# Fewer, larger loads, loads moved behind a transposition, and sums one unit ahead, in a top-k attention and gated MLP kernel

## Chip, core and metric

The kernel runs on one core of a Trainium2 chip. The metric is device time in microseconds: the median of three runs for the times, and one profiled execution for the views. An engine is written as in the profile: PE is TensorE (PEld its weight loads), DVE is VectorE, ACT is ScalarE, POOL is GpSimd, SP is SyncE, which here issues nearly all DMAs (SPq is its sequencer).

## The reference

Attention over 8 batches of 8 heads, 576 positions of 64 elements. Only the 32 largest scores of each row count. The result, seen as 4608 rows of 512, goes through two matrix products with a gate between them.

```python
scores = scale * np.matmul(q, k.transpose(0, 1, 3, 2))
kth = np.partition(scores, -top_k, axis=-1)[..., -top_k:-top_k + 1]
scores = np.where(scores >= kth, scores, -1000000000.0)
attn = np.exp(scores - np.max(scores, axis=-1, keepdims=True))
attn = attn / (np.sum(attn, axis=-1, keepdims=True) + 1e-09)
attn_out = np.matmul(attn, v)
x = attn_out.transpose(0, 2, 1, 3).reshape(4608, 512)
h = x @ w_in                               # 512 -> 2048
g = h * (1.0 / (1.0 + np.exp(-1.702 * h)))
out = g @ w_out                            # 2048 -> 512
```

## The kernel before

**Slots.** The attention is cut into 144 slots, 18 for each batch. A full slot is one pair of heads (hp, 0 to 3) against 128 of the first 512 query rows; two slots of a batch hold the ends, the last 64 rows of two pairs at once. Batches of even number run their 16 full slots first and then the two slots of ends; odd ones begin with the ends. All four pairs of v are therefore read in the last two slots of an even batch and in the first two of an odd one.

**A slot's way.** PE makes the scores (L315), ACT copies them to SBUF as `sc` (copy_scores, L327). DVE halves them into pairs (pair_up, L337) and finds the 32 largest by MAX8 and MATCH_REPLACE8 (L351, L355). POOL makes bounds, ACT masks and takes exponentials into `pr` (L382, L390), DVE inverts the sums (L398, L400), POOL scales `pr` (normalize, L413). `split(n)` (L449, L451) copies `pr` on ACT into two planes of 16 bits, over the slot's own `sc`, and SP writes them to DRAM as `rows`. `turn_by_dma(n)` (L457) has SP read them back transposed as `pt`; that DMA waits until `rows` has landed and until PE has read the `pt` of two slots before, since there are two buffers. Then PE multiplies by v (`values_at`, L516), and ACT copies the result to `xT` (x_of, L530 or L533). `sc` has four buffers, so copy_scores of slot n + 4 waits until `rows` of slot n has landed.

**The MLP** runs between the slots in units of four groups of 128 hidden features: `hidden` on PE (L573), `tanh` on ACT (L589), `gate` (on POOL, or on DVE at L604 when the attention is done), `combine` (four sums for a seven-product scheme, L626 to L629) and `project` on PE (L680). The units go through lists in order of arrival: to_gate, gated, to_combine, to_project. The tiles `th`, `h` and `sums` come from one pool of eight. When a block's four units are projected, ACT takes the sums from PSUM (L698), the parts are added (L705) and SP writes four pieces to `out_dram` (L714).

**The order** is written out by hand. After an opening and the slots up to 12, `two_slots(n)` is called for n = 13, 15, ... 145; one call, a trip here, does the odd slot n and the even slot n + 1 of DVE's search, and `values_at` for slots n - 3 and n - 2. Below n = 21 (`filling`) its second loads come before the scores of n + 3; from there on they come near the end, between `split(n)` and `turn_by_dma(n)`. After the last trip, `last_units` empties the lists.

**Loads.** `at(n, fn, ...)` notes what is due at a slot; `begin(0)` in a trip runs what is due at n, between `split(n - 1)` and `turn_by_dma(n - 1)`, and `begin(1)` what is due at n + 1. All loads and the transpositions are issued by SP in that one order. A pair's q is fetched at FETCH, which from batch 2 on falls on begin(0), and its k one slot later, on begin(1): each is two transfers of 128 KB (L196), one for each head, and one of 32 KB for the ends (L199). At READY, `prepare_by_dma` has ACT copy the pair into two planes (`halves`, L264), SP write them to DRAM (`qk_rows`, L268 to L273), and SP read them back transposed as `qk_t` (L277), which the scores read. FETCH is -17, -13, -9 and -5 slots before the batch, READY -13, -9, -5 and -1, but in odd batches -3 for the last pair. v is loaded by `load_v` for one pair at a time: 256 KB into one of four buffers (L210) and two transfers of 16 KB for the ends into a tile of zeros (L218). VALUES says when: slots 0, 1, 2 and 3 of an even batch, and all four pairs at slot 2 of an odd one, which is begin(1) of the trip at its slot 1 (n = 19, 55, 91 and 127).

Of the kernel before, what the change touches and what calls it, by code (L numbers as in the profile page):

```python
# [11 lines left out]
F32 = mybir.dt.float32  # L12
# [6 lines left out]
P = 128  # L19
# [11 lines left out]
def kernel(  # L31
# [64 lines left out]
    pool = lambda name, bufs, **kw: ctx.enter_context(tc.tile_pool(name=name, bufs=bufs, **kw))  # L96
    raws = const.tile([P, RING, 2 * PIECE], U32, name="raws")
    loads = pool("loads", 1)
    vals = pool("vals", 4)
    qkt = pool("qkt", 6)  # L100
    scp = pool("scp", 4)
    prp = pool("prp", 2)
# [62 lines left out]

    qT, kT, vv = {}, {}, {}
    loaded = {}
    v_ends = [const.tile([P, 2, D], F32, name=f"v_e{i}") for i in range(NP)]
    for i, t in enumerate(v_ends):
        (nc.gpsimd if i else nc.vector).memset(t[:], 0.0)  # L170

    def stay_warm(count, of=ident[:]):

# [4 lines left out]
    def load(name, b, hp, queue=None):  # L178

        src = q if name == "q" else k  # L180
        if (b, hp) not in loaded:
            home, tag = (ptp, "pt") if b == 0 and hp % 2 else (prp, "pr") if b == 0 and hp else (loads, "qk_l")
            if b == 1 and hp % 2:
                parts = raws[:, 3, :].bitcast(F32), diagonals[:, 0, :]
                loaded[b, hp] = [x.rearrange("p (t j d) -> p t j d", j=2, d=D) for x in parts]
            else:
                t = home.tile([P, 2 * NF + 1, 2, D], F32, name="qk_l", tag=tag)
                loaded[b, hp] = [t[:, 0 : 2 * NF, :, :], t[:, 2 * NF :, :, :], t]
        t = loaded[b, hp]
        if queue is None:  # L190
            heads_of = lambda j: of_load(name, t)[:, :, j, :]
        else:
            heads_of = lambda j: heads_apart(name, t)[:, j, :, :]
        queue = queue or nc.sync
        for j in range(2):
            queue.dma_start(heads_of(j), src[b, 2 * hp + j, 0:FULL, :].rearrange("(p t) d -> p t d", t=NF))  # L196

        on = slice(0, TAIL) if name == "q" else slice(TAIL, P)
        queue.dma_start(t[1][on, 0, :, :], src[b, 2 * hp : 2 * hp + 2, FULL:S, :].rearrange("h p d -> p h d"))  # L199
# [5 lines left out]
        flat = of_load(name, t).rearrange("p t j d -> p (t j d)")  # L205
        return flat.rearrange("p (j t d) -> p j t d", j=2, t=NF)

    def load_v(b, hp):
        main = vals.tile([P, 2, NF, D], F32, name="v_l")
        nc.sync.dma_start(  # L210
            main[:].rearrange("p j t d -> p j (t d)"),
            v[b, 2 * hp : 2 * hp + 2, 0:FULL, :].rearrange("j (p t) d -> p j (t d)", t=NF),
        )


        tail = v_ends[(b * NP + hp) % len(v_ends)]
        for j in range(2):
            nc.sync.dma_start(tail[j * TAIL : (j + 1) * TAIL, j, :], v[b, 2 * hp + j, FULL:S, :])  # L218
        vv[b, hp] = main, tail

    def prepare_main(name, b, hp):
        src = loaded[b, hp]
# [522 lines left out]
    READY_1 = (-5, -5, -3, -3)  # L745
    FETCH = (-17, -13, -9, -5)
    FETCH_1 = (-11, -6, -4, -4)
    VALUES = (0, 1, 2, 3), (2, 2, 2, 2)
    by_slot = dict(enumerate([2, 2, 3, 3, 3, 3, 3, 3, 3, 3, 3, 1]))
    for n in by_slot:  # L750
        first = sum(map(len, list(by_slot.values())[:n]))
# [10 lines left out]
    for b in range(1, B):  # L762
        for hp in range(NP):
            if b > 1:
                for i, name in enumerate("qk"):
                    at(b * PER + FETCH[hp] + i, load, name, b, hp)
                at(b * PER + READY[b % 2][hp], prepare_by_dma, b, hp)
            else:
                at(b * PER + FETCH_1[hp], load_both, b, hp)
                at(b * PER + READY_1[hp], prepare_by_pe, b, hp)  # L770
            at(b * PER + VALUES[b % 2][hp], load_v, b, hp)
    unfinished = []
    early = []
    finished = []
# [36 lines left out]

    def opening():

        stay_warm(8, v_ends[0][:].rearrange("p j d -> p (j d)"))
        load("q", 0, 0, nc.sync)
        load("k", 0, 0, nc.scalar)
        for hp in range(2):
            for name in "qk":
                if hp:
                    load(name, 0, hp)  # L820
        for x in by_slot[0]:
            load_piece(x)
        prepare_first()
        scores(0)
        copy_scores(0)
        stay_warm(2)
        for name in "qk":
            prepare(name, 0, 1)
        early.extend(round_piece(x) for x in by_slot[0])
        for piece in early:  # L830
            piece["size"]()
        scores(1)
        copy_scores(1)
        prepare_rest()
        for hp in range(2, NP):
            for name in "qk":
                load(name, 0, hp)
        load_v(0, 0)
        for x in by_slot[1]:
            load_piece(x)  # L840
# [180 lines left out]
    def two_slots(n):  # L1021

        begin, prepare_some = dues(n)
        aside = n < N
        filling = n < STEADY + 8
        if live(n - 1):
            exponentials(n - 1)
        if n == STEADY:
            prepare_some()
        hidden(ps_t)  # L1030
        if n > STEADY + 2:
            hidden(ps_t)
# [12 lines left out]
        gate()  # L1045
        begin(0)
        if live(n - 1):
            turn_by_dma(n - 1)
        while turns:
            turns.pop(0)()  # L1050
        if live(n + 2):
            copy_scores(n + 2)
        if live(n):
            bounds(n)
            mask(n)
        combine()
        project_one()
        sum_weights(4)
        if live(n):
            exps(n)  # L1060
        tanh(aside)
        prepare_some()
        prepare_some()
        held = [m for m in (n - 3, n - 2) if live(m)]
        o = ps_t.tile([P, 4, P], F32, name="o", tag="tp") if held else None
        ends = [(b, hp, o[:, 2 + i, :]) for i, (b, hp) in enumerate(second_part)]
        second_part.clear()
        for what in ends:
            turn_qk_ends(*what)
        for i, m in enumerate(held):  # L1070
            values_at(m, o[:, i, :])
        if filling and held:
            x_of(held, o)
        for what in ends:
            copy_qk_ends(*what)
        if filling:
            begin(1)
        if live(n + 3):
            scores(n + 3)
        leave_all()  # L1080
        find(n + 1, 8)
        if live(n):
            normalize(n)
            split(n)
        if held and not filling:
            x_of(held, o)
        if not filling:
            begin(1)
        if live(n):
            turn_by_dma(n)  # L1090
        gate()
        if live(n + 3):
            copy_scores(n + 3)
        if live(n + 1):
            bounds(n + 1)
        sum_weights(4)
# [11 lines left out]
    with tc.manual_schedule():  # L1108
# [3 lines left out]
        first_pair(PAIRED)  # L1112
        for n in range(STEADY, N + 2, 2):
            two_slots(n)
        while ready or to_gate or gated or to_combine or to_project:
            last_units()
        merge_all(nc.vector)
# [30 lines left out]
```

## Time and profile before

| | us |
|---|---|
| median of three runs | 1448.03 (1445.33 to 1450.77) |
| profiled execution, its own time | 1444.36 |
| its span, first to last instruction | 1442.4 |
| PE busy in the span | 1380.9 |
| DVE busy | 1343.8 |
| ACT busy | 1163.7 |
| POOL busy | 959.3 |

The page's 40 slices show PE and DVE at nine tenths or more from about 250 us on, and the last two slices with PE alone. A row of waits names the engine that stood, the line that it stood before, what ended the wait, the total in us, the number of times and the longest. In a timeline a row has start, length, engine, line and what is written and read; for SP the length is the time to issue, and the landing is told apart. The page's part on DMAs gives the median from issue to landing: 3.6 us for `rows`, 4.9 for `pt`, 5.4 for `qk_t`, 3.8 for 256 KB of v, 3.4 to 3.5 for 128 KB of q or k.

### The profile page before, as it was taken

What the parts mean: (1) busy time and instruction counts of PE and PEld (TensorE: products, weight loads), DVE (VectorE), ACT (ScalarE), POOL (GpSimd) and SP (SyncE); (2) the same over time, 40 slices, a digit from 0 to 9 for tenths busy, and PEclk for the clock granted to TensorE, in tenths of its full rate; (3) what the DMA queues carried; (4) which work ended last, traced back from release to release, by engine and by line L of the source; (5) the groups of instructions that cost most, each with busy time, mean ns of one, the idle gap of its engine ahead of it and who ended that gap; (6) DMA issues with size and microseconds to landing.
All of it is one profiled execution on the core that took longest, in us unless ns stands there. A gap on an engine that the chain in (4) does not pass through costs nothing. (4 is left out here: it accounts for less than half of the span.)

```text
span 1442.4 us, 45910 instructions
## 1 busy us (share of the span) xinstructions
PE 1380.9 (96%) x18164; PEld 1234.5 (86%) x18164; DVE 1343.8 (93%) x3521; ACT 1163.7 (81%) x1896; POOL 959.3 (67%) x1608
## 2 busy tenths in 40 slices
PE   6889799999999999999999999999999999999996
PEld 5667478899999899899899999889999998899986
DVE  7999998999999999999999999999999999999812
ACT  6998777888888888888888898888888888888811
POOL 4787676677777667666677767667777767777710
PEclk8899899999999999999999999999999999999999
DMA  7452456777787786777787786787798877655520
GB/s 225 137 156 67 132 146 149 193 191 192 181 203 193 176 217 168 175 190 188 186 212 190 189 197 169 190 196 191 183 203 195 191 184 182 173 141 141 140 58 16
DMA packets 535991, 245.47 MB, mean 170 GB/s; under 512 B 458976, under 2 KB 514272, under 8 KB 535776
## 3 DMA queue, kind: packets, MB, share of 16 engines
q1 hardware_dynamic: 535344, 242.25, 67.1%
q8 instruction: 142, 2.33, 0.7%
q14 instruction: 73, 0.60, 0.1%
q10 hardware_dynamic: 432, 0.30, 0.1%
HBM read 45.09 MB, written 103.42 MB: 103 GB/s over the span
## 5 line engine op out<-in xcount | busy, mean ns | idle before, releaser
L351 DVE MAX8 top<-ranked 128x8 f32<-128x288 f32 (+1 forms) x1080 | 598.8, 596 | 0.0
L573 PEld LDWEIGHTS ph<-xT,win 128*128 128x128 f32 x4384 | 496.0, 193 | 30.6 <-issue 17.4
L573 PE MATMUL ph<-xT,win 128*128 128x128 f32 x4384 | 509.7, 278 | 0.0
L355 DVE MATCH_REPLACE8 ranked<-top,ranked 128x288 f32<-128x288 f32 (+1 forms) x810 | 433.5, 543 | 0.0
L413 POOL TENSOR_SCALAR pr<-pr,rden 128x576 f32<-128x576 f32 x268 | 197.0, 745 | 337.7 <-DVE rden L400 156.3
L449 ACT COPY sc<-pr 128x2304 uint16<-128x2304 uint16 x134 | 283.4, 2115 | 140.5 <-POOL pr L413 140.2
L337 DVE TENSOR_TENSOR ranked<-sc 128x576 f32<-128x576 f32 x270 | 219.6, 854 | 11.4 <-ACT sc L327 11.4
L390 ACT ACTIVATE pr<-sc,low 128x576 f32<-128x576 f32 x288 | 220.3, 773 | 0.0
L382 ACT ACTIVATE sc<-sc,cut 128x576 f32<-128x576 f32 x288 | 207.9, 779 | 4.5 <-POOL cut L369 4.5
L680 PE MATMUL po<-wout,h 128*64 128x128 f32 x2064 | 200.7, 273 | 0.2
L680 PE MATMUL po<-raws,h 128*64 128x128 f32 x2064 | 200.6, 273 | 0.2 <-POOL h L627 0.2
L327 ACT ACTIVATE sc<-s_ps 128x576 f32<-128x576 f32 x288 | 171.5, 650 | 26.2 <-DMA rows<-sc 19.1
L315 PE MATMUL s_ps<-qk_t 64*64 64x288 f32 x2304 | 181.3, 429 | 1.1 <-DMA qk_t<-qk_rows 0.8
L602 POOL TENSOR_TENSOR th<-th,h 128x512 f32<-128x512 f32 x131 | 167.7, 1280 | 10.9
L680 PE MATMUL po<-wout,th 128*64 128x128 f32 x2176 | 168.6, 276 | 0.0
L516 PE MATMUL o<-pt,v_l 128*64 128x128 f32 (+1 forms) x2400 | 146.0, 266 | 12.2 <-DMA pt<-rows 12.2
L680 PEld LDWEIGHTS po<-wout,th 128*64 128x64 f32 x2176 | 124.3, 137 | 28.4 <-issue 15.3
L516 PEld LDWEIGHTS o<-pt,v_l 128*64 128x64 f32 x2400 | 127.8, 140 | 14.2 <-issue 8.6
L680 PEld LDWEIGHTS po<-wout,h 128*64 128x64 f32 x2064 | 130.3, 137 | 0.9 <-POOL h L628 0.9
L680 PEld LDWEIGHTS po<-raws,h 128*64 128x64 f32 x2064 | 130.4, 137 | 0.6 <-POOL h L627 0.4
L315 PEld LDWEIGHTS s_ps<-qk_t 64*64 64x64 f32 x2304 | 77.1, 136 | 50.4 <-issue 14.8
L705 POOL TENSOR_TENSOR raws<-raws 128x128 f32<-128x128 f32 (+1 forms) x165 | 92.0, 566 | 37.1 <-ACT raws L698 29.3
(106 smaller groups left out, 1720.4 us busy)
## 6 DMA issues: line engine op xcount, KB each, us to landing
rows<-sc SPq DMA_DIRECT2D x134, 576.0 KB, 3.6
qk_rows<-halves SPq DMA_DIRECT2D x48, 256.0 KB, 2.9
out_dram<-raws SPq DMA_DIRECT2D x136, 64.0 KB, 2.3
raws<-in_moe_w_in_dram SPq DMA_DIRECT2D x16, 512.0 KB, 4.5
v_l<-in_v_dram SPq DMA_DIRECT2D x32, 256.0 KB, 3.8
raws<-in_moe_w_out_dram SPq DMA_DIRECT2D x16, 512.0 KB, 3.5
qk_l<-in_q_dram SPq DMA_DIRECT2D x60, 128.0 KB, 3.4
qk_l<-in_k_dram SPq DMA_DIRECT2D x58, 128.0 KB, 3.5
```

The lines of the kernel that those rows point to most:

```text
L315: nc.tensor.matmul(ps[i][rows, c, 0:HALF], lhsT=qT[b, hps[p]][on, cols], rhs=kT[b, hps[p]][on, FIRST[i] + c * HALF : FIRST[i] + (c + 1) * ...
L327: nc.scalar.mul(out=to, in_=ps[i][:, :, 0:HALF], mul=SCALE)
L337: nc.vector.tensor_tensor(out=ranked[n][:, :, c, :], in0=a, in1=b, op=op)
L351: nc.vector.max(top[:, i, 8 * r : 8 * r + 8], of(r, i))
L355: nc.vector.match_replace(to, top[:, i, 8 * r : 8 * r + 8], of(r, i), LOWEST)
L382: nc.scalar.activation(sc[:, i, :], sc[:, i, :], AF.Prelu, bias=cut[:, i : i + 1], alpha=HUGE)
L390: nc.scalar.activation(pr[:, i * S : (i + 1) * S], sc[:, i, :], AF.Exp, bias=low[:, i : i + 1], accum_out=den[:, i : i + 1],)
L413: nc.gpsimd.tensor_scalar(pr[:, i, :], pr[:, i, :], st[n]["rden"][:, i : i + 1], 1.0, op0=ALU.mult, op1=ALU.mult)
L449: nc.scalar.copy(out=halves, in_=pr[:].bitcast(U16).rearrange("p (k h) -> p h k", h=2))
L516: nc.tensor.matmul(o[j * D : (j + 1) * D, cols], lhsT=main[:, j, c, :] if c < NF else tail[:, j, :], rhs=pt[:, MAIN[j] + c if c < NF else ...
L573: nc.tensor.matmul(ph[:, i * P : (i + 1) * P], lhsT=win[:, c, f * P : (f + 1) * P], rhs=xs[:, x.place, c, :], start=(c == 0), stop=(c == C ...
L680: nc.tensor.matmul(both_banks[y * TAIL : (y + 1) * TAIL, bank, r * P : (r + 1) * P], lhsT=a[:, i, :], rhs=weight(w, fs[i])[:, y * P : (y + ...
```

## The change

- `load_v` takes several pairs. v lies in one constant tile, `v_main`, for all four pairs, the ends in one tile `v_tail`. One main transfer and two for the ends serve all pairs named. VALUES loads pairs 0 and 1 at slot 0 and 2 and 3 at slot 2 of an even batch, and all four at slot 2 of an odd one. In batch 0 the pairs are still loaded one by one.
- `load` for batches 2 and later moves q or k of both heads by one transfer of 256 KB in place of two of 128 KB. The transfer for the ends stays.
- In `two_slots`, from n = 21 on, `turn_by_dma(n)` comes before `begin(1)` and no longer after it.
- One `combine()` stands before the loop over `last_units`.

In all SP issues 102 transfers fewer. The instructions of the other engines are the same; in the tail the added `combine` moves DVE's sums one unit ahead of its gates.

```diff
-    vals = pool("vals", 4)
+    v_main = const.tile([P, NP, 2, NF, D], F32, name="v_l")
...
-    v_ends = [const.tile([P, 2, D], F32, name=f"v_e{i}") for i in range(NP)]
-    for i, t in enumerate(v_ends):
-        (nc.gpsimd if i else nc.vector).memset(t[:], 0.0)
+    v_tail = const.tile([P, NP, 2, D], F32, name="v_e")
+    for i in range(NP):
+        (nc.gpsimd if i else nc.vector).memset(v_tail[:, i, :, :], 0.0)
...
-        for j in range(2):
-            queue.dma_start(heads_of(j), src[b, 2 * hp + j, 0:FULL, :].rearrange("(p t) d -> p t d", t=NF))
+        if b > 1:
+            both = src[b, 2 * hp : 2 * hp + 2, 0:FULL, :].rearrange("j (p t) d -> p t j d", t=NF)
+            queue.dma_start(of_load(name, t), both)
+        else:
+            for j in range(2):
+                queue.dma_start(heads_of(j), src[b, 2 * hp + j, 0:FULL, :].rearrange("(p t) d -> p t d", t=NF))
...
-    def load_v(b, hp):
-        main = vals.tile([P, 2, NF, D], F32, name="v_l")
+    def load_v(b, *hps):
+        pairs, heads = slice(hps[0], hps[-1] + 1), slice(2 * hps[0], 2 * hps[-1] + 2)
         nc.sync.dma_start(
-            main[:].rearrange("p j t d -> p j (t d)"),
-            v[b, 2 * hp : 2 * hp + 2, 0:FULL, :].rearrange("j (p t) d -> p j (t d)", t=NF),
+            v_main[:, pairs, :, :, :].rearrange("p h j t d -> p (h j) (t d)"),
+            v[b, heads, 0:FULL, :].rearrange("j (p t) d -> p j (t d)", t=NF),
         )
-        tail = v_ends[(b * NP + hp) % len(v_ends)]
         for j in range(2):
-            nc.sync.dma_start(tail[j * TAIL : (j + 1) * TAIL, j, :], v[b, 2 * hp + j, FULL:S, :])
-        vv[b, hp] = main, tail
+            nc.sync.dma_start(
+                v_tail[j * TAIL : (j + 1) * TAIL, pairs, j, :],
+                v[b, heads.start + j : heads.stop : 2, FULL:S, :].rearrange("h p d -> p h d"),
+            )
+        for hp in hps:
+            vv[b, hp] = v_main[:, hp, :, :, :], v_tail[:, hp, :, :]
...
-    VALUES = (0, 1, 2, 3), (2, 2, 2, 2)
+    VALUES = {(0, 1): 0, (2, 3): 2}, {(0, 1, 2, 3): 2}
...
-            at(b * PER + VALUES[b % 2][hp], load_v, b, hp)
+        for hps, n in VALUES[b % 2].items():
+            at(b * PER + n, load_v, b, *hps)
...
         if held and not filling:
             x_of(held, o)
+        if live(n):
+            turn_by_dma(n)
         if not filling:
             begin(1)
-        if live(n):
-            turn_by_dma(n)
...
         for n in range(STEADY, N + 2, 2):
             two_slots(n)
+        combine()
         while ready or to_gate or gated or to_combine or to_project:
             last_units()
```

More of the change, by code (lines that the diff above doesn't have):

```diff
@@ L812, in opening @@
     def opening():
-        stay_warm(8, v_ends[0][:].rearrange("p j d -> p (j d)"))
+        stay_warm(8, v_tail[:, 0, :, :].rearrange("p j d -> p (j d)"))
         load("q", 0, 0, nc.sync)
```

## The prediction

> **What bounds the kernel now.** I read the page's busy shares first, then its chain of waits, the busy time by stage, the waits by engine, and last the timeline of SP's queue around them. In the fence are the page's first part, the chain's shares and one stage of 100 us (length, then PE, weight loads, DVE, ACT, POOL, granted clock, DMA share, GB/s):
>
> ```profile
> PE 1380.9 (96%) x18164; PEld 1234.5 (86%) x18164; DVE 1343.8 (93%) x3521; ACT 1163.7 (81%) x1896; POOL 959.3 (67%) x1608
> PE ph L573 6%; PE po L680 5%; PE o L516 2%; PE s_ps L315 1%; DMA pt<-rows 0%; DVE top L351 0%; DVE ranked L355 0%; ACT th L589 0%; DVE th L604 0%; DMA qk_l<-in_k_dram 0%; ACT pr L390 0%; POOL raws L705 0%; ACT sc L449 0%; ACT sc L382 0%; DVE ranked L337 0%
> 300.00:400.00 100.00, 100.00 (x1377) 91.65 (x1376) 99.62 (x266) 87.80 (x138) 70.58 (x125) 1.00 0.77 189
> ```
>
> The chain reaches back to 1176 us, and 14 of its 18 per cent are PE. In the steady part PE and DVE are both full at a granted clock of 1.00. A trip of two_slots takes PE 7.34 (ph) + 6.26 (po) + 2.18 (o) + 2 x 1.13 (s_ps) = 18.04 us by the chain of waits, and DVE has 0.4 us free in 100. So neither makes good a stall, and the end is PE's own work plus PE's waits, each of which the next view shows (engine, waited for: us, times, longest):
>
> ```profile
> PE o L516 <- DMA pt<-rows: 12.2, 7, 4.2
> PE po L680 <- DVE sums L627: 6.8, 5, 1.4
> PE s_ps L315 <- DMA qk_t<-qk_rows: 0.8, 1, 0.8
> ACT sc L327 <- DMA rows<-sc: 19.1, 13, 5.1
> ACT halves L264 <- DMA qk_l<-in_k_dram: 5.8, 3, 3.6
> ```
>
> The seven waits for pt stand at 255.90 (4.16), 494.03 (0.88), 587.17 (2.45), 698.22 (0.76), 916.30 (1.03), 955.14 (2.20) and 1247.47 (0.76). Each is for the odd slot of a trip in which loads stood in SP's queue between rows<-sc and the transposition. At 587 the queue shows it:
>
> ```profile
> 569.37 0.58 SPq L451 DMA_DIRECT2D rows<-sc  x1
> 570.00 0.43 SPq L210 DMA_DIRECT2D v_l<-in_v_dram  x1
> ...
> 578.81 1.26 SPq L196 DMA_DIRECT2D qk_l<-in_k_dram  x2
> 580.11 0.63 SPq L199 DMA_DIRECT2D qk_l<-in_k_dram  x1
> 580.79 4.16 SPq L457 DMA_TRANSPOSE pt<-rows  x1
> 585.04 2.69 SPq L714 DMA_DIRECT2D out_dram<-raws  x4
> 587.83 0.54 SPq L451 DMA_DIRECT2D rows<-sc  x1
> ```
>
> Rows landed 3.6 us after 569.37; the transposition began 7.8 us later than that. Everything behind it was late too: the next rows went out 9.3 us after their copy had ended, and DVE stood for 2.8.
>
> **The change by parts.** I keep two clocks: P, PE's stream, and Q, the stream of DVE, ACT and SP, both as change against before (minus is earlier). P waits for Q only for pt and qk_t.
>
> *One transfer for v, one for both heads, at slots 18 and 19 (before the loads move).* At 236.02 to 246.18 SP issued 12 v and 3 k transfers, while rows(19) had been ready since 238.03. After: 0.44 + 2 x 0.59 (v) + 0.63 + 0.70 (k) = 2.95 us, 7.2 less, if a large transfer issues like a small one. The other end: the longest issue of any row, 4.16 for a transposition, in place of the first 0.44 leaves a saving of 3.5, 0.7 short of the wait. I take the first, since what the large ones move is no more than before. PE's 4.16 goes, and DVE's 3.58 + 0.74 + 1.01 + 0.74. ACT's score copies start within 0.1 us of PE's scores in other trips, and DVE has 1.3 to spare there, so I let Q gain 5.5. P -4.2, Q -5.5.
>
> *k's loads behind the transposition, ordinary trips.* It removes PE's 0.88 + 0.76 + 2.20: rows land in 3.0 us where no load follows them and in 3.5 to 5.4 where one does, pt in 4.5 to 4.7 against 6.1. Bounds 0 and 3.8; I take all. DVE's stalls there give Q -1.1. The loads now stand behind the transposition's wait for rows (283.6 us in 122 waits on SP, 2.3 each) and its issue of 2.6, and their own two issues (1.3 us) are no longer hidden inside that wait. Behind them on SP are out_dram, qk_rows and the even slot's rows; pt of even slots lands some 10 us before PE wants it, so this costs nothing. Without that cover it is 1.3 a trip.
>
> *v at slots 55, 91, 127.* The other three pt waits, 4.24, go, and with them DVE's 2.8 and 1.9: P -4.2, Q -4.7. New: 1 MB lands behind the transposition. It can issue at about 573.0 + 2.6 = 575.6 and PE reads it from 583.4; by the landing rows (256 KB 3.8, at most 6.8) there are between 4 and 1 us to spare, less what P has gained on Q. I allow 0 to 2 us of wait, thrice, and take 0, as the next step decides the end.
>
> *The price: the third pairs' k.* In batches 3, 5 and 7 the last pair is prepared (READY -3) one trip after its k is fetched (FETCH -5 and -4), and ACT already waits for that k:
>
> ```profile
> 515.70 0.52 SPq L451 DMA_DIRECT2D rows<-sc  x1
> 516.28 1.64 SPq L196 DMA_DIRECT2D qk_l<-in_k_dram  x2
> 517.96 0.73 SPq L199 DMA_DIRECT2D qk_l<-in_k_dram  x1
> 519.27 2.61 SPq L457 DMA_TRANSPOSE pt<-rows  x1
> 520.62 2.11 ACT L264 COPY halves<-qk_l 128x2304 uint16<-128x2304 uint16 x1 [1.06 <-DMA qk_l<-in_k_dram]
> 524.65 1.18 ACT L327 ACTIVATE sc<-s_ps 128x576 f32<-128x576 f32 x2
> 525.94 1.42 DVE L337 TENSOR_TENSOR ranked<-sc 128x576 f32<-128x576 f32 x2
> ```
>
> After: rows at 515.70, landed 3.2 later (518.9), transposition to 521.5, k issued 521.6 and 522.2, landed 2.8 after the last issue (525.0). Halves start 4.4 late. Behind them on ACT stand a split and the score copies, and DVE begins 0.1 us after those: DVE stands 4.3 to 4.4. Bounds: 2.24 for the transposition, 2.3 for a landing make 3.5; 4.16, 2.33 to issue and 5.5 to land make some 10. I take 4.4 because the queue there is the ordinary one.
> Third place by Q: -5.5 - 1.1 - 4.7 + 2 x 4.4 = -2.5. There the last qk_t landed at 1200.97 and PE, stopped for 0.79, went on at 1201.10. After: 1200.97 - 2.5 + 4.4, so PE goes on 1.9 later than before; what P had gained is lost there. Behind it only the 0.76 at 1247 remains to be gained: P +1.1.
>
> The Trainium skill ("DMA: Bandwidth & Descriptors", Rules for kernel authors) speaks against this move: issue a DMA early and wait for it late. With the loads left early at those three places the sum would hold P's full -13.0 instead of +1.1. The same page (Anatomy of one DMA) fits a transfer, on another issuing path, with 2.0 us plus bytes over 436 GB/s: 2.7 us for k's 288 KB, as the row has it; no run here shows that fit.
>
> *Sums ahead in the tail.* Five times PE stops 1.35 to 1.41 us between po's first 8 matmuls and the rest, for sums made after a gate that waits for the hidden just done. With one unit ahead, sums for a project exist when its hidden ends; the last unit's tanh, gate and sums take 0.60 + 0.69 + 1.2 behind a project of 3.06, so it is covered as well. P -6.8.
>
> **Sum.** Profiled execution 1444.36 (span 1442.4): +1.1 - 6.8 = -5.7, 1438.7. The median shown is 1448.03, 3.7 more; forecast 1442.3.
>
> **Rivals.** (a) *The late k is hidden*, lands early or DVE's stall is swallowed: odd slots of quiet trips have pt 6 to 7 us before PE wants it. Then all 13.0 + 6.8 go: 1428. Against it: at 1183 a 3.64 wait for k became 2.67 on DVE and 0.79 on PE. (b) *Large transfers clog SP's queue* at those places: k lands by the upper bound, 10 late instead of 4.4, adding 3 x 5.9 = 17.7: 1460, slower. It passes the old time from 6.3 us late (3 x 1.9 = 5.7). For it: at 483.5 a second k transfer took 2.33 to issue and 4.9 to land. Against it: that was behind a rows transfer still under way, and the landings of 5.5 are of the opening. (c) *The queue is not what it seems*, the waits move elsewhere and only the tail gains: 1441.
>
> **Chances.** Forecast 0.46, own range 1436 to 1449 (k late by 3.5 to 5.5, Q's gains 3 us out either way); (a) 0.20; (c) 0.20; (b) 0.14. Half a per cent, about what a measurement of this kernel tells from none, is 7.2 us: faster means under 1440.8, which (a) and some 0.23 of the forecast and (c) reach; slower over 1455.3, (b). Faster 0.43, same 0.43, slower 0.14. Range 1430 to 1454.
>
> **What would show it.** After: no wait of PE's for pt over 1 us at the places above; none of po for sums; halves waiting for k three times, about 5.5, 5.5 and 8 us, each with a DVE stall of 4 or more and a PE wait for qk_t; SP issuing v in about 2 us. Halves' total under 10, or no wait for qk_t, makes me wrong towards (a).

## The result, and the profile after

The changed kernel took 1457.99 us in the median of four runs (1454.63 to 1460.08), the kernel before 1447.64 beside it (1445.33 to 1450.77): a ratio of 1.0068, interval 1.0041 to 1.0095. The change costs some 10 us, where the forecast was a gain of 6. The profiled execution took 1460.08 (span 1458.3). Line numbers after are 5 higher than before in the slot's code: 337 is 342, 516 is 521.

The page's first part shows that no engine has more instructions. PE's 8.6 us more of busy time fit its clock, which stands at half for 17.1 us more than before (below):

```profile
PE 1389.5 (95%) x18164; PEld 1237.4 (85%) x18164; DVE 1345.9 (92%) x3521; ACT 1163.5 (80%) x1896; POOL 960.5 (66%) x1608
```

The waits of PE, ACT and DVE after (engine, waited for: us, times, longest):

```profile
PE s_ps L320 <- ACT sc L332: 8.2, 3, 4.0
PE ph L578 <- ACT h L597: 5.8, 3, 2.6
PE o L521 <- DMA pt<-rows: 5.2, 4, 2.2
...
ACT sc L332 <- DMA rows<-sc: 30.2, 24, 2.6
ACT halves L269 <- DMA qk_l<-in_k_dram: 24.9, 3, 9.8
...
DVE ranked L342 <- ACT sc L332: 31.3, 15, 8.9
```

Most of what was to go has gone: PE's wait for pt fell from 12.2 to 5.2, though its longest is still 2.2, and its 6.8 for sums in the tail is no longer listed. What the forecast feared is there and larger: halves wait for k 24.9 us in three places (5.8 before). The first two rows are new: PE waits 14.0 us for copies of ACT, in the trips of these three places; for qk_t, where the forecast had it stop, it waits 2.1 us. One row has grown that the forecast did not speak of: ACT's copies of the scores wait for `rows` in 24 places, not 13, and for 30.2 us, not 19.1.

The first of the three places, in the timeline of SP, ACT and DVE (start, length, engine, line; in brackets the idle time before it):

```profile
516.95 0.52 SPq L456 DMA_DIRECT2D rows<-sc  x1
520.23 2.70 SPq L462 DMA_TRANSPOSE pt<-rows  x1
522.98 0.64 SPq L197 DMA_DIRECT2D qk_l<-in_k_dram  x1
523.67 0.69 SPq L203 DMA_DIRECT2D qk_l<-in_k_dram  x1
...
526.60 2.11 ACT L269 COPY halves<-qk_l 128x2304 uint16<-128x2304 uint16 x1 [7.50 <-DMA qk_l<-in_k_dram]
...
530.63 1.19 ACT L332 ACTIVATE sc<-s_ps 128x576 f32<-128x576 f32 x2
...
531.85 1.43 DVE L342 TENSOR_TENSOR ranked<-sc 128x576 f32<-128x576 f32 x2 [6.49 <-ACT sc L332]
```

The transposition starts with the landing of the rows, k is issued when it is done, and ACT, DVE and then PE stand until k has landed: the shape that the forecast drew, with a halves wait of 7.50 in place of some 5.5. PE's clock in the 12 us behind it (window, length, then busy time of PE, weight loads, DVE, ACT, POOL; granted clock, DMA share, GB/s):

```profile
531.00:535.00 4.00, 1.73 (x16) 0.69 (x16) 2.38 (x6) 4.00 (x9) 0.00 (x0) 0.90 0.98 270
535.00:539.00 4.00, 3.34 (x15) 3.34 (x16) 4.00 (x10) 3.75 (x6) 3.68 (x7) 0.50 1.03 219
539.00:543.00 4.00, 4.00 (x30) 4.00 (x29) 4.00 (x13) 4.00 (x10) 3.69 (x8) 0.75 1.07 229
```

At 534.2, after one gap of PE and within a second (1.53 and 2.60 us), the granted clock falls to 0.50, for 6.83 us. From 230 us to the tail it stands at 0.5 for 27.3 us after and for 10.2 before.

Where the time went is best read from one mark: the start of PE's first product with `pt` of slot n. The table gives it for the profiled executions, against the kernel before (minus is earlier). The three tight places lie between 47 and 51, 83 and 87, 119 and 123; the other rows belong to experiments told below.

| slot | 19 | 39 | 47 | 51 | 83 | 87 | 119 | 123 | 143 | end of PE |
|---|---|---|---|---|---|---|---|---|---|---|
| changed kernel | -4.5 | -4.8 | -1.6 | 5.7 | 6.5 | 16.5 | 17.8 | 24.9 | 24.2 | 15.8 |
| loads_ahead | -5.4 | -6.3 | -5.6 | -3.7 | -9.1 | -9.1 | -12.8 | -12.3 | -13.1 | -21.5 |
| three_ahead | -2.0 | -3.4 | 0.4 | 4.7 | 3.4 | 7.3 | 9.2 | 11.6 | 10.6 | 2.2 |
| refilled | -2.3 | -4.6 | -1.1 | 5.3 | 4.2 | 11.7 | 12.7 | 19.3 | 18.6 | 10.1 |
| outs_in_wait | -3.6 | -5.9 | -6.4 | -5.6 | -10.9 | -10.9 | -14.8 | -16.6 | -16.6 | -25.0 |
| after_outs | -4.3 | -6.6 | -7.2 | -3.6 | -8.9 | -5.3 | -9.2 | -5.1 | -5.9 | -14.3 |
| ahead_outs | -4.6 | -6.9 | -8.0 | -8.0 | -13.3 | -13.3 | -17.2 | -19.4 | -20.2 | -28.6 |

The changed kernel gains 4.5 by slot 19, as forecast, loses 7.3, 10.0 and 7.1 at the tight places, and gives up some more between them. The tail gains 8.4. A profiled execution need not be a middling one: that of three_ahead was the slowest of its ten runs (1446.49; the fastest took 1430.13), that of the changed kernel the slowest of four. The medians below decide.

### The profile page after: what moved, and what is told of

Read it like the earlier page. It is cut to its first block, busy times and chain, and to the rows that moved or that the text cites. A ratio compares the mean times of both kernels' runs of the same rounds, so it can differ in the third digit from the quotient of the medians.

```text
span 1458.3 us, 45771 instructions
## 1 busy us (share of the span) xinstructions
PE 1389.5 (95%) x18164; PEld 1237.4 (85%) x18164; DVE 1345.9 (92%) x3521; ACT 1163.5 (80%) x1896; POOL 960.5 (66%) x1608
## 5 line engine op out<-in xcount | busy, mean ns | idle before, releaser
L578 PEld LDWEIGHTS ph<-xT,win 128*128 128x128 f32 x4384 | 501.8, 194 | 37.0 <-issue 25.8
L578 PE MATMUL ph<-xT,win 128*128 128x128 f32 x4384 | 515.5, 279 | 5.8 <-ACT h L597 5.8
L332 ACT ACTIVATE sc<-s_ps 128x576 f32<-128x576 f32 x288 | 171.8, 651 | 37.7 <-DMA rows<-sc 30.2
L320 PE MATMUL s_ps<-qk_t 64*64 64x288 f32 x2304 | 182.6, 428 | 10.6 <-ACT sc L332 8.2
L607 POOL TENSOR_TENSOR th<-th,h 128x512 f32<-128x512 f32 x131 | 167.9, 1282 | 10.9
L685 PEld LDWEIGHTS po<-wout,th 128*64 128x64 f32 x2176 | 124.2, 137 | 28.8 <-POOL pr L418 14.9
L320 PEld LDWEIGHTS s_ps<-qk_t 64*64 64x64 f32 x2304 | 77.9, 136 | 61.2 <-issue 17.1
```

Of the source, the lines that this page charges most:

```text
L320: nc.tensor.matmul(ps[i][rows, c, 0:HALF], lhsT=qT[b, hps[p]][on, cols], rhs=kT[b, hps[p]][on, FIRST[i] + c * HALF : FIRST[i] + (c + 1) * ...
L332: nc.scalar.mul(out=to, in_=ps[i][:, :, 0:HALF], mul=SCALE)
L578: nc.tensor.matmul(ph[:, i * P : (i + 1) * P], lhsT=win[:, c, f * P : (f + 1) * P], rhs=xs[:, x.place, c, :], start=(c == 0), stop=(c == C ...
L685: nc.tensor.matmul(both_banks[y * TAIL : (y + 1) * TAIL, bank, r * P : (r + 1) * P], lhsT=a[:, i, :], rhs=weight(w, fs[i])[:, y * P : (y + ...
```

## The experiments

The kernel before took 1444.01, 1447.45, 1446.75 and 1440.42 beside the four groups of runs, so ratios are compared between groups; 0.0010 of a ratio is 1.4 us. A difference of two runs is known to some 0.002 to 0.005, 3 to 7 us. The groups are loads_ahead to tail_alone, v_alone to small_ahead, v_first to filled, and refilled to ahead_outs.

| run | what it is | us | ratio to before, interval |
|---|---|---|---|
| changed kernel | | 1457.99 | 1.0068 [1.0041, 1.0095] |
| loads_ahead | changed, without the move | 1422.30 | 0.9847 [0.9819, 0.9874] |
| three_ahead | move in ordinary trips only | 1440.00 | 0.9960 [0.9938, 0.9981] |
| move_alone | before, with the move | 1489.53 | 1.0297 [1.0264, 1.0330] |
| tail_alone | before, with the tail's combine | 1436.40 | 0.9948 [0.9925, 0.9971] |
| v_alone | before, with v merged | 1433.44 | 0.9913 [0.9882, 0.9944] |
| qk_alone | before, with q and k merged | 1442.85 | 0.9979 [0.9959, 0.9998] |
| small_behind | loads_ahead, two small writes behind | 1432.73 | 0.9908 [0.9877, 0.9938] |
| small_ahead | loads_ahead, the same writes ahead | 1424.98 | 0.9855 [0.9823, 0.9887] |
| v_first | three_ahead, v ahead too | 1430.70 | 0.9899 [0.9861, 0.9937] |
| outs_in_wait | three_ahead, output writes in a wait | 1420.45 | 0.9813 [0.9788, 0.9838] |
| k_with_q | loads_ahead, tight k earlier still | 1425.26 | 0.9847 [0.9820, 0.9873] |
| filled | changed, PE's gaps filled, first attempt | 1473.29 | 1.0179 [1.0153, 1.0205] |
| refilled | changed, PE's gaps filled | 1453.37 | 1.0085 [1.0065, 1.0105] |
| after_outs | changed, output writes in a wait | 1431.62 | 0.9937 [0.9919, 0.9956] |
| ahead_outs | loads_ahead, output writes in a wait | 1416.48 | 0.9834 [0.9818, 0.9849] |

### The parts by themselves

The first four runs weigh three causes: the late k in the three tight trips, transfers that clog the queue by their size, and the order on SP in the ordinary trips.

**loads_ahead**

```diff
-        if live(n):
-            turn_by_dma(n)
         if not filling:
             begin(1)
+        if live(n):
+            turn_by_dma(n)
```

> The changed kernel with begin(1) ahead of turn_by_dma(n) again; v, q/k and the tail stay changed. Theory 1 (the late k of the last pairs of batches 3, 5 and 7 costs the time: three DVE stalls of 6 to 9 us, and PE stalls with a halved clock behind them): the three waits of halves for k fall back to about 1, 1 and 4 us, and the time falls below the kernel before, to about 1430 (tail 6.8, the waits at slots 19, 55, 91 and the halved clock at 255 some 10). Theory 2 (the large transfers themselves clog SP's queue): halves still wait long, and the time stays above 1447.

1422.30, 0.9847. All other parts stay, and the kernel is 2.2 per cent (32 us, 0.0221 of 1447) faster than the changed one. The move is a loss as a whole, and the rest of the change a gain of 22. The kernel is some 8 us faster than the 1430 that was expected. The two waits that stood out fall, in the waits of ACT of this kernel:

```profile
ACT sc L332 <- DMA rows<-sc: 6.9, 7, 2.2
ACT halves L269 <- DMA qk_l<-in_k_dram: 6.4, 3, 3.4
```

**three_ahead**: the loads ahead again, but only in trips 49, 85 and 121, which fetch the third pairs' k (hp 3).

```diff
+        tight = n % (2 * PER) == PER - 5
+        if not filling and tight:
+            begin(1)
         if live(n):
             turn_by_dma(n)
-        if not filling:
+        if not filling and not tight:
             begin(1)
```

> The changed kernel, with begin(1) ahead of turn_by_dma(n) only in the trips n = 49, 85 and 121, which fetch the k that is wanted one trip later. Theory 1: as the run with loads ahead everywhere, about 1430, or some us better since the ordinary trips keep the move. Theory 3 (the move costs in every trip that has loads, since their issues no longer lie inside the wait for rows, so that the next slot's rows go out late): the three large stalls go, some 20 us, but small waits of PE for pt and of ACT for rows stay; about 1438, slower than with all loads ahead.

1440.00, 0.9960. The three trips are worth 0.0108 or 15.6 us, and 0.0113 or 16.4 us stay: about half of the move's price is paid in trips where no k was needed soon.

**move_alone**: the move in the kernel before, and nothing else.

```diff
+        if live(n):
+            turn_by_dma(n)
         if not filling:
             begin(1)
-        if live(n):
-            turn_by_dma(n)
```

> The kernel before with only the move of begin(1) behind turn_by_dma(n). Theory 1: three waits of halves of 6 us or more, three stalls of PE with a halved clock, against the pt waits at 587, 916 and 955 saved: about 1460. Theory 2: no slower than before, 1440 to 1448.

1489.53, 1.0297, 43 us lost. Without the merged loads, and so with more and smaller transfers behind the transposition, the move costs more, not less. That speaks against the size of the transfers. It is also more than either theory had, 1460 and 1440 to 1448: 72 issues of v and 69 of k lie behind a transposition here, and rows go out 4.0 us late in the mean, by the measure given below.

**tail_alone**: the tail's part in the kernel before.

```diff
             two_slots(n)
+        combine()
         while ready or to_gate or gated or to_combine or to_project:
```

> The kernel before with only the combine ahead of the loop over last_units. All theories: PE's five waits for sums in the tail (6.8 us) go and nothing else changes: 1440.8.

1436.40, 0.9948, a gain of 7.5 us of 1447, where the forecast's step said 6.8.

**v_alone and qk_alone**: in the kernel before, only the change's `load_v` with its tiles, or only its `load`. At the core of each:

```diff
-    VALUES = (0, 1, 2, 3), (2, 2, 2, 2)
+    VALUES = {(0, 1): 0, (2, 3): 2}, {(0, 1, 2, 3): 2}
...
+            both = src[b, 2 * hp : 2 * hp + 2, 0:FULL, :].rearrange("j (p t) d -> p t j d", t=NF)
+            queue.dma_start(of_load(name, t), both)
```

> The kernel before with v alone merged: one transfer for v of two or four pairs and one for each half of its remainders (12 issues to 3 in an odd batch, to 6 in an even one); q and k head by head as before, the loads ahead of the transposition, no sums made ahead in the tail. Without the move the changed kernel took 1422.3 and the tail's part alone was worth 7.6, so v and q/k together are worth some 14. Theory 'SP's time' (what counts is the time that SP's issues take outside a wait for rows): v's twelve issues at slots 2 of the odd batches are 12 x 0.62 = 7.4 us ahead of one transposition, twice the 3.3 to 4.5 that its rows need, and so v has most of the gain: 1430 to 1437 (-7 to -14). Rival 'the gain is in q and k' (each load one issue shorter at some 24 trips): v alone 1440 to 1446.

> The kernel before with both heads of q or k in one transfer, and nothing else. Theory 'SP's time': a load of three issues is 2 us and lies inside the wait for rows (3.3 to 4.5), so to save one of the three saves SP little there: 1440 to 1446 (0 to -4). Rival 'the gain is in q and k': 1430 to 1437. If both v and q/k alone give -10 or more, they relieve the same thing and do not add up.

v alone gives 0.0087 (12.6 us) and q and k 0.0021 (3.0 us). With the tail's 0.0052 that is 0.0160, and loads_ahead has 0.0153: the parts add up. v has most of it; that this is owed to its twelve transfers of an odd batch, which stood ahead of one transposition, is likely but was not told apart from its even batches.

### Why the ordinary trips pay

In three_ahead SP has in one ordinary trip, one that fetches v and a k (start, length to issue, line; the ACT row is the copy that makes the next rows):

```profile
406.53 0.53 SPq L456 DMA_DIRECT2D rows<-sc  x1
409.65 2.11 ACT L454 COPY sc<-pr 128x2304 uint16<-128x2304 uint16 x1 [1.58 <-POOL pr L418]
410.28 2.51 SPq L462 DMA_TRANSPOSE pt<-rows  x1
412.83 0.57 SPq L214 DMA_DIRECT2D v_l<-in_v_dram  x1
...
415.44 1.04 SPq L203 DMA_DIRECT2D qk_l<-in_k_dram  x1
416.58 1.31 SPq L456 DMA_DIRECT2D rows<-sc  x1
```

and loads_ahead in the same trip:

```profile
401.09 0.53 SPq L456 DMA_DIRECT2D rows<-sc  x1
401.71 0.40 SPq L214 DMA_DIRECT2D v_l<-in_v_dram  x1
...
404.80 0.70 SPq L203 DMA_DIRECT2D qk_l<-in_k_dram  x1
406.01 3.72 SPq L462 DMA_TRANSPOSE pt<-rows  x1
406.72 2.11 ACT L454 COPY sc<-pr 128x2304 uint16<-128x2304 uint16 x1 [1.58 <-POOL pr L418]
409.83 0.53 SPq L456 DMA_DIRECT2D rows<-sc  x1
```

From rows to the next rows SP takes 10.05 us in three_ahead and 8.74 in loads_ahead. Between rows and transposition SP waits for the landing in either case, 3.2 us idle in the one, with a landing 3.7 us after the issue; in the other the loads' 3.8 us of issue lie in it, and the landing took 4.9. In three_ahead the issues stand on their own behind the transposition, 3.7 us from 412.83 to the next rows. ACT had ended the copy for those rows at 411.76, so they go out 4.8 us late, and all behind them on SP is late too; in loads_ahead they go out 1.0 late.

How late, the trace tells over the whole run: the time from the end of a split's copy on ACT to the issue of its rows, as a mean over slots 30 to 137. The columns to the right of it are the time, as a ratio to before, and the part of SP's order that differs.

| kernel | rows late, us | ratio | differs from loads_ahead by |
|---|---|---|---|
| loads_ahead | 2.2 | 0.9847 | |
| small_ahead | 2.3 | 0.9855 | two writes inside the wait |
| k_with_q | 2.7 | 0.9847 | tight k beside q, one slot earlier |
| v_first | 2.9 | 0.9899 | k behind, but in tight trips |
| small_behind | 3.0 | 0.9908 | two writes behind |
| three_ahead | 3.6 | 0.9960 | k and v behind, but in tight trips |
| changed kernel | 3.7 | 1.0068 | k and v behind |
| outs_in_wait | 1.7 | 0.9813 | as three_ahead, output writes in a wait |
| ahead_outs | 1.0 | 0.9834 | output writes in a wait |
| after_outs | 1.3 | 0.9937 | k and v behind, output writes in a wait |

The means come from one profiled execution each, the ratios from medians. Where the tight trips are ahead, the time follows this mean roughly, down to some 2 us and no further; k_with_q does not fit, with rows later than in loads_ahead at the same time. Who waits for the late rows is in the waits of three_ahead:

```profile
ACT sc L332 <- DMA rows<-sc: 29.4, 27, 2.3
DVE ranked L342 <- ACT sc L332: 14.7, 14, 3.3
PE o L521 <- DMA pt<-rows: 7.4, 5, 2.9
PE ph L578 <- ACT h L597: 3.5, 3, 1.9
```

and of loads_ahead, where ACT's wait for rows is 6.9 (above):

```profile
DVE ranked L342 <- ACT sc L332: 5.7, 5, 2.1
PE o L521 <- DMA pt<-rows: 1.6, 1, 1.6
```

ACT's copy of later scores waits for the rows, DVE's search for the copy, and PE for the `pt` of odd slots, which then comes late. Between 230 and 1350 us PE idles 16.2 us in three_ahead and 5.0 in loads_ahead, and its clock is halved for 13.7 us and not at all. The runs told next changed it with transfers that carry next to nothing, and with transfers that are no loads.

**small_behind and small_ahead**: loads_ahead with two small writes in each trip that fetches a k. The first of the two new calls in the diff is that of small_ahead, the second that of small_behind; each kernel has one.

```diff
+    def two_small():
+        for i in range(2):
+            nc.sync.dma_start(spare[i], ident[:, 0:32].rearrange("p (a b) -> p a b", a=2))
...
         if not filling:
             begin(1)
+        if not filling and fetching:
+            two_small()
         if live(n):
             turn_by_dma(n)
+        if not filling and fetching:
+            two_small()
```

> The changed kernel with the loads ahead of the transposition again (1422.3 before), and in each trip that fetches a k two more issues on SP's queue, right behind the odd slot's transposition, where the move had put k's: 128 bytes from each of 128 partitions to a spare place in DRAM that nothing reads, some 0.6 us of SP each and next to no data. Theory 'SP's time': the price of the move in the ordinary trips is the 1.3 us of SP that no longer lie in a wait for rows, whatever they carry; so this costs about what the ordinary trips cost when only the three last fetches went ahead (1440.0): 1434 to 1443. Rival 'the data' (k lands late, or moves at the same time as the next rows and the transposition): two small writes cost nothing, 1420 to 1427.

> The same two small writes, but issued ahead of the odd slot's transposition, behind k's load, while SP waits for the rows. Theory 'SP's time': k's two issues and these are 2.6 us, less than the 3.3 to 4.5 of the wait, so they are covered: 1420 to 1428; in the two trips of an even batch that also issue v it is more than the wait, 1 to 2 us each. Rival 'any further issue costs, wherever it stands': the same as behind, 1434 to 1443.

Behind: 1432.73, 0.0061 or 8.8 us more than loads_ahead. Ahead: 1424.98, 0.0008 or 1.2 us more, within the intervals. 46 issues of 24.6 us in all cost 8.8 us of the kernel outside a wait for rows and nothing that can be told inside one. The two ran in one group and do not overlap (1429.60 to 1434.09, 1422.69 to 1429.49). There is no k in them and hardly a byte: 16 KB each. The expectation for behind, 1434 to 1443, was a little too high. The 8.8 are half of what three_ahead lost against loads_ahead; v, which the move also put behind, is told apart next.

**v_first**: three_ahead, with v's transfers ahead as well; `begin` is given the function that it is to run.

```diff
-        if not filling and tight:
-            begin(1)
+        if not filling:
+            begin(1, load if tight else load_v)
         if live(n):
             turn_by_dma(n)
-        if not filling and not tight:
-            begin(1)
+        if not filling:
+            begin(1, load_v if tight else load)
```

> The kernel with only the three tight fetches ahead of the transposition (1440.0 before), and v's transfers ahead of it too: behind it remain k's two issues in 21 trips. Theory 'SP's time': in that kernel 42 issues of k (35 us) and 27 of v (20 us) lay behind a transposition, and it took 16 to 18 more than with all of them ahead; the two small writes, 46 issues of 25 us, took 9 more. At 0.3 to 0.36 us for each us, k's 35 us cost 11 to 13: 1432 to 1437. Rival 'k's data' (k alone is what matters): 1438 to 1442. Rival 'v's transfers are what costs': 1421 to 1428.

1430.70, 0.9899. It lies between the 1432 to 1437 that was expected from SP's time and the 1421 to 1428 of the rival that v's transfers are what costs. Of the 16.4 us of the ordinary trips v's 27 issues have 0.0061 (8.8 us) and k's 40 have 0.0052 (7.5 us), each known to some 6 or 7 us. So no price of k's data shows beyond that of the small writes: 32 us of issue for k cost 7.5, 24.6 for the small writes cost 8.8. v's 18 us cost as much as k's 32, perhaps since three transfers and k's two often stand there together; that wasn't tried further, nor whether v's data has a price.

**outs_in_wait**: three_ahead, its k and v still behind. Only the four writes of a finished block to `out_dram` are held back from where `merge_all` issues them, and go out ahead of the even slot's transposition.

```diff
-                    nc.sync.dma_start(rows[:, :, y, :], parts[y * TAIL : (y + 1) * TAIL, :, :])
+                    to, of = rows[:, :, y, :], parts[y * TAIL : (y + 1) * TAIL, :, :]
+                    going.append(lambda to=to, of=of: nc.sync.dma_start(to, of))
...
         begin(0)
+        go()
         if live(n - 1):
             turn_by_dma(n - 1)
```

> The kernel with only the three tight fetches ahead (1440.0), its k and v still behind the transposition, but the four writes of each finished block of the output (136 issues, 95 us of SP's time outside the waits for rows) issued ahead of the even slot's transposition, behind q's load. Theory 'SP's time': SP gets back more than the 55 us that the move took, so the ordinary trips' price goes although no load is where it was: 1422 to 1430; q's load (1.6 us) and four writes (2.4) are about a wait for rows (3.3 to 4.5). Rival 'the loads' place' (k late, or its data beside the next rows): 1437 to 1442.

1420.45, 0.9813: faster than three_ahead by 0.0147 (21 us), with every load where three_ahead has it. Its queue in a trip with such writes:

```profile
429.80 0.57 SPq L456 DMA_DIRECT2D rows<-sc  x1
430.41 0.65 SPq L197 DMA_DIRECT2D qk_l<-in_q_dram  x1
431.10 1.17 SPq L203 DMA_DIRECT2D qk_l<-in_q_dram  x1
432.37 3.14 SPq L720 DMA_DIRECT2D out_dram<-raws  x4
435.62 2.56 SPq L462 DMA_TRANSPOSE pt<-rows  x1
```

The fence shows q's load and four writes between the rows and their transposition. That wait is not for rows alone: the transposition of an even slot also waits until PE has read the `pt` of two slots before, and began 0.7 us after its rows had landed (the median of slots 30 to 137; 2.1 in ahead_outs). ACT's wait for rows is no longer among its longest waits, and PE idles 1.4 us between 230 and 1350. With this the cause in the ordinary trips is shown from both sides: time of issue put outside the wait slows the kernel also where it carries next to nothing, and other time of issue put into the wait wins the loss back.

### Why the tight places pay so much

**k_with_q**: loads_ahead, with k of the third pairs one slot earlier, beside q in the even slot's wait.

```diff
-                    at(b * PER + FETCH[hp] + i, load, name, b, hp)
+                    at(b * PER + FETCH[hp] + (0 if b % 2 and hp == 3 else i), load, name, b, hp)
```

> The kernel with all loads ahead of the transposition (1422.3), and in the three tight fetches k one slot earlier, right behind q, both in the even slot's wait for rows. Theory 'SP's time': q and k are 3 us, less than that wait; k lands some 9 us earlier, ACT's wait for it (6.4 us in three places) and DVE's (5.7 us) go, PE's gaps there too: 1417 to 1422. Rival 'PE has the rest' (PE idles 3 us in all between 250 and 1150, and waits of ACT and DVE are slack): no difference, 1420 to 1426.

1425.26, 0.9847: no difference from loads_ahead. ACT no longer waits for k at all, so the remaining 6.4 us of that wait cost nothing that shows. A late k seems to cost from some point on, not from its first microsecond; but rows went out somewhat later here (2.7 against 2.2 us), and a small gain may have been lost by that.

**filled and refilled**: products of a constant that nothing reads, where PE stood idle in the tight places of the changed kernel. The diff is that of refilled; filled had other counts, and wrote both fills into the tile of `o`.

```diff
+    def fill(count, to):
+        for _ in range(count):
+            nc.tensor.matmul(to, lhsT=ident[:], rhs=ident[:], start=True, stop=True)
...
+        if n in FILL:
+            fill(FILL[n][0], o[:, 3, :])
         if live(n + 3):
             scores(n + 3)
+        if n in FILL:
+            fill(FILL[n][1], st[n + 3]["ps"][1][:, 1, 3 * P : 4 * P])
```

> The changed kernel, and at the three places of the late k PE gets products of a constant that nothing reads (into free columns of a bank) where it stood idle: 12, 20 and 30 of 128x128 ahead of the scores in trips 51, 87 and 123 (gaps of 1.53, 2.65 and 3.97 us), and 20, 12 and 12 ahead of the next trip's first hidden block (2.60, 1.60, 1.63); at 0.11 us each they fill 1.3 to 3.4 us. Nothing of SP's order changes, the halves are as late as before. Theory 'the clock': of what the three places cost, the stretches of granted clock 0.5 that follow PE's gaps (6.83, 10.24 and 6.83 us) take half their length, 12 us; without gaps of 2 us the clock stays at 1.0: 1446 to 1452. Rival 'the waits': the time is lost in ACT's wait for k, and PE is not what is waited for afterwards: 1456 to 1462.

1473.29, 1.0179, and no answer: a product took 0.245 us and not 0.11, so the first fill was about twice as long as its gap, and the second waited 4.6, 3.1 and 3.5 us for ACT's copy of `o`, whose tile it wrote. It delayed PE by itself.

> The fill of PE's gaps again, with its two faults out: a product of 128x128 takes 0.245 us, so there are 6, 10 and 15 ahead of the scores of trips 51, 87 and 123 (gaps of 1.53, 2.65 and 3.97 us), and the second fill, 9, 5 and 5 products, goes right behind these scores into free columns of their own bank, where nothing waits (gaps of 2.60, 1.60 and 1.63), not behind ACT's copy of o. All else is the changed kernel. Theory 'the clock': the granted clock stays at 1.0, and half of the 23.9 us that it stood at 0.5 comes back: 1446 to 1452. Rival 'the waits': what is lost is lost in ACT's wait for k, and PE's speed afterwards changes nothing: 1456 to 1462.

1453.37, 1.0085, no less than the changed kernel's 1.0068: at the 1447 of the other groups some 1459, in the range of the rival. The fill did what it should for the clock. The first place of refilled by windows, to be held against those above:

```profile
531.00:535.00 4.00, 4.00 (x43) 3.26 (x41) 2.53 (x6) 4.00 (x10) 0.00 (x0) 1.00 0.99 270
535.00:539.00 4.00, 3.74 (x34) 3.55 (x33) 4.00 (x10) 3.75 (x6) 3.84 (x7) 1.00 1.07 220
```

The clock is 1.00 in these windows, and between 230 us and the tail it was never halved. Yet the three places cost 6.4, 7.5 and 6.6 by the table, 20.5 in place of 24.4. Of the 12 us that half clock should have cost there 4 came back in the profiled execution, and none that the runs can tell. So the half clock is for the greater part a companion of the loss, not its cause; whether the products themselves hold PE up a little was not told apart.

**after_outs**: the changed kernel with all its second loads behind the transposition, as it has them, and the output's writes in the wait as in outs_in_wait. **ahead_outs**: the same, with all loads ahead. The one differs from the other by:

```diff
-        if live(n):
-            turn_by_dma(n)
         if not filling:
             begin(1)
+        if live(n):
+            turn_by_dma(n)
```

> The changed kernel with all its second loads behind the transposition, as it is, and only the four writes of a finished block moved into the even slot's wait for rows. In the ordinary trips that took 1440.0 to 1420.5. Theory 'SP's time in all places': also the three tight fetches are late by SP's order, k's halves wait 3 to 5 us in place of 7.5 to 9.8, and most of the three places' price (some 18) goes too: 1421 to 1430. Rival 'the tight fetches are late by their own place' (k is issued behind the odd slot's transposition, 4 to 5 us later, whatever SP did before): the three places keep their 14 to 20: 1434 to 1442.

> All loads ahead of the transposition (1422.3), and the four writes of a finished block in the even slot's wait for rows: a version that beats both kernels, if the two add up. Theory 'PE has the rest': with only the tight fetches ahead and the writes moved, PE idled 1.4 us between 230 and 1350 and ACT waited for no rows; there is nothing left for SP's order to give, so this is the same: 1418 to 1424. Rival 'SP still counts': the loads' 44 us inside the waits as well give another 5 and more: 1410 to 1416.

after_outs has 0.9937, ahead_outs 0.9834, on the same chip: the move costs 0.0103, 14.9 us, when SP has time. By the table nearly all of it lies in the tight places: from 47 to 51, 83 to 87 and 119 to 123 after_outs loses 3.6, 3.6 and 4.1, ahead_outs 0, 0 and -2.2, so 13.5 us. Halves wait for k in after_outs:

```profile
ACT halves L269 <- DMA qk_l<-in_k_dram: 15.8, 3, 6.7
```

In ahead_outs it is 2.0 in two places, so the wait for k is 13.8 us longer in three places, 4.6 in each. That is the rival of after_outs: the tight fetches are late by their own place. ahead_outs and outs_in_wait do not differ by their intervals; in ahead_outs PE idles 0.2 us from 230 to 1350, so SP's order has hardly anything left to give there. Both are faster than the kernel before and than the changed kernel, by 1.7 to 1.9 and by 2.3 to 2.6 per cent of before.

## Why the prediction was wrong, step by step

- **One transfer for v, one for both heads, and v at slots 55, 91 and 127.** Right as the gain of P: the sum of these steps, of the ordinary trips' waits and of the one wait for qk_t was 13.0 before the price, and loads_ahead, which has them without the move, stands 13.1 earlier at slot 143. But of that sum 3.84 was written to the move, and it came without it.
- **k's loads behind the transposition, ordinary trips.** This is the step that failed. The prediction said of k's two issues that they "are no longer hidden inside that wait", that behind them stand the even slot's rows, and that "pt of even slots lands some 10 us before PE wants it, so this costs nothing". pt of even slots does stay well ahead of PE, by 8.7 us in the median in the changed kernel (10.7 before) and never by less than 5.4. But the rows that are late are waited for by another: `sc` has four buffers, and ACT's copy of the scores waits until rows have landed. What ACT is late, DVE's search is late, and with it the `pt` of the odd slots, for which PE has less to spare. So the step should have moved Q later, and it moved it 1.1 earlier. The prediction had the signs before it: ACT's wait for rows, 19.1 us in 13 places, stands in its fence, and around 587 it read rows that went out 9.3 us late and a DVE that stood for 2.8. The price that it named for the case without cover, 1.3 a trip, would have been 26 us in 20 trips. The runs show 16.4 (three_ahead against loads_ahead), of which k has some 7.5, and v 8.8, whose issues the forecast moved too and priced by their landing alone. The premise that P waits for Q "only for pt and qk_t" did not hold either: in the ordinary trips PE's waits are mostly for pt (7.4 us in three_ahead, 3.5 for `h`), but in the tight places of the changed kernel they are 14.0 us for ACT's copies.
- **The price: the third pairs' k** (those of hp 3). That k would come late, and its own size, were right: 4.4 a place forecast, 13.2 on Q and 14.1 on P in all; 4.6 longer waits and 13.5 us measured where SP has time (after_outs against ahead_outs). The last link was not: PE stood before the scores and `hidden` for ACT's copies, and hardly for qk_t. In the changed kernel k's halves wait 18.5 us more than in loads_ahead, 6.2 in each place, and the places cost 24.4 by the table against 2.4 there and 11.3 in after_outs: SP's lateness adds to the late k.
- **Sums ahead in the tail.** Right: 6.8 forecast, 7.5 measured.
- **The sum.** The forecast of 1442.3 and the ordinary trips' 16.4, which it had at nothing, make 1458.7; 1457.99 was measured. That it fits to 0.7 is in part luck: the gain without the move was 22 where the forecast's steps had 19.8, the three trips cost 15.6 where they had 14.1, and these two misses cancel.
- **Rivals.** The late k hidden (1428) fell: k costs 13.5. The tail alone (1441) fell: the merged loads gain 15.6 (v_alone and qk_alone together). The queue clogged by large transfers (1460) has the time, by luck, but not the cause. At 6.1 to 6.6 against before the halves are not 10 late, move_alone is worse without large transfers, and small writes cost the same. Of the signs that were named, halves' total of 24.9 seemed to confirm the forecast's own mechanism, and the waits for pt of up to 2.2 us, where none over 1 was to be, spoke against it; none was a sign of the late rows as such. In the trace of before rows already went out 2.8 us late in the mean, by the measure above.
- **The rule.** The Trainium skill ("DMA: Bandwidth & Descriptors", Rules for kernel authors) says to issue a DMA early and wait for it late. The runs agree: the loads behind the transposition cost 32 us in this kernel. What decided, though, was not only the wait for the data but the issuing time of SP: 24.6 us of small writes cost 8.8.

## What to carry to other kernels

A queue that waits in order for a landing has free time in that wait: see what issues fit into it, and count every issue that leaves it, also where nobody waits for its data. When a stall is declared covered, follow each consumer of what comes late, the buffers' reuse too; here it was not the reader of `pt` but the writer of the next `sc`. A change of three parts is best measured in parts: two gained 22 us here and the third lost 32.

## What the runs showed of the hardware

- SP's time of issue is a resource of its own. In the changed kernel, from 230 us to the tail, a transposition of `rows` took SP 2.6 us in the median (2.3 to 3.7), one of `qk_rows` 3.0 (2.3 to 4.6); most plain transfers took 0.5 to 0.7, single ones up to 2.3. It hardly went by size: a write of 16 KB (small_behind) took 0.58 in the median, a load of 256 KB of k 0.64, one of 512 KB or 1 MB of v 0.58.
- The granted clock halved after gaps of PE of 1.98 us (three_ahead, at 456.8) and 2.17 us (changed kernel, at 454.7), and did not after one of 2.40 (refilled, at 493.0); in three_ahead it also halved at a gap of 1.52 (at 1211.8). So the length of one gap didn't decide it, and the 2 us in the expectation of filled are no threshold. Up to the tail the stretches last 3.41 us or twice or three times that. What does decide it was not tried.
